# A clustered attention and two MoE layers: a one-hot maximum kept in PSUM, and 1e-9 added by a sum instead of a scalar add

## The chip, the core and the metric

The kernel runs on one core of a Trainium2 chip. The metric is the device time of one execution in microseconds. A core has a matrix engine (TensorE, PE in the rows; its weight loads are listed as PEld), a vector engine (VectorE, DVE), a scalar engine (ScalarE, ACT), a general engine (GpSimd, POOL) and a queue that issues DMAs (SyncE, SP). Each takes its own instructions strictly in order, and they meet at semaphores. SBUF is the large on-chip memory, PSUM the memory that TensorE writes its results into.

## The reference

Three stages follow each other: attention masked by clusters, a dense two-layer MoE expert with a gated unit, and a top-2 MoE over eight experts. The change is in the first alone.

```python
q_assign = np.argmax(np.einsum('bhsd,hcd->bhsc', q_n, c_n), axis=-1)
k_assign = np.argmax(np.einsum('bhsd,hcd->bhsc', k_n, c_n), axis=-1)
mask = q_assign[:, :, :, None] == k_assign[:, :, None, :]
scores = scale * np.matmul(q, k.transpose(0, 1, 3, 2))
scores = np.where(mask, scores, -1000000000.0)
scores = scores - np.max(scores, axis=-1, keepdims=True)
attn = np.exp(scores)
attn = attn / (np.sum(attn, axis=-1, keepdims=True) + 1e-09)
return np.matmul(attn, v).astype(np.float32)
```

There are 2 batches, 8 heads, 768 positions of 64 numbers and 16 clusters.

## The kernel before, in words

**Tiling.** Attention works on eight units, each one batch and one pair of heads. A unit has 12 steps: three groups of query rows (qp), two heads (h), two blocks of 128 rows (i). In a step TensorE makes the scores of 128 queries against 768 keys in two halves (`scores`, L397 and L398), VectorE takes the row maximum (`rowmax`, nm, L403), ScalarE the exponential with its row sum beside it (`expo`, L411), TensorE transposes it (L420), ScalarE and VectorE split it into a high and a low part (PTh, L430; PTl, L435), and TensorE multiplies both with v (`pv`, L455).

**Beside the steps** of one unit the next unit is prepared. Its q and k are transposed and split, their similarity to the clusters is made (simT, then sim in the PSUM tile ps_m, L324), and from that comes a one-hot of the first largest cluster, all on 128 x 384 numbers (24 groups of 16 clusters): the maximum of a group (`c_max`, L330), a compare with it (`c_eq`, L336), a product with falling ranks (`c_rank`, L342, on GpSimd except for the first unit), the maximum of the ranks (`c_first`, m2, L346), and two compares of rank with m2 that write the one-hot oh, one half each (`c_hot`, L353). TensorE transposes oh in six pieces (`h_tr`, L360) into the next user of ps_m, and ScalarE copies it out; four DMAs put it under the q and k operands as the mask.

**The division** runs once per group of query rows, so 24 times: `o_inv` adds 1e-9 to four sums (L480) and takes the reciprocal (L481) into r; GpSimd spreads r over a tile (L485), TensorE transposes that, and GpSimd multiplies it in.

**Order.** A table (TIMES) gives each operation a due time in steps; sorted by it, the operations are written out by hand for all five engines. After attention a scheduler orders what is not written out, the loads of the first dense-layer weights (si, so; L701, L703) and their decoding (L121 to L131) among it. The scores' tile, the transposed tile and the exponential have two buffers each; ps_m has one.

Of the kernel before, what the change touches and what calls it, by code (L numbers as in the profile page):

```python
# [8 lines left out]
F32 = mybir.dt.float32  # L9
# [6 lines left out]
OP = mybir.AluOpType  # L16
AX = mybir.AxisListType
# [3 lines left out]
NCL = 16  # L21
NB = S // 128
# [88 lines left out]
def f(ap):  # L111
    return ap.bitcast(F32)
# [21 lines left out]
class Attention:  # L134
# [52 lines left out]
    def s_set(self):  # L187
        nc = self.nc
        self.ch = self.C([128, H, 2, 2, NCL], F32R, "ch")
        nc.gpsimd.memset(f(self.ch), 0.0)  # L190
        self.zc = self.C([128, 2, 2, 224], F32R, "zc")
        nc.gpsimd.memset(f(self.zc), 0.0)
        self.rev = self.C([128, NCL], F32, "rev")
        nc.gpsimd.iota(self.rev, pattern=[[-1, NCL]], base=NCL, channel_multiplier=0,
                       allow_small_or_imprecise_dtypes=True)
        sb = self.ohsb = self.C([64, 2], F32, "ohsb")
        for p, i, x in ((32, 0, 1.0), (0, 0, PEN), (32, 1, 0.0), (0, 1, -PEN)):
            nc.vector.memset(sb[p:p + 32, i:i + 1], x)
        self.did("set")
# [118 lines left out]
        self.nc.scalar.activation(sT.rearrange("p a n -> p (a n)"), self.t.pop(("simT", u)), AF.Copy)  # L318

    def c_tr(self, u):  # L320
        sim = self.t["sim", u] = self.psm(u, [128, 3, 4, 2, NCL])
        sT = self.t.pop(("sT", u))
        for j in range(3):
            self.nc.tensor.transpose(sim[:, j].rearrange("p g i n -> p (g i n)"), sT[:, j], self.ident)  # L324
# [6 lines left out]

    def c_eq(self, u):
        G = NB * 4
        sv = self.t.pop(("sim", u)).rearrange("p j g i n -> p (j g i) n")
        eq = self.t["eq", u] = self.sm.tile([128, G, NCL], F32, tag="eq", name="eq", bufs=1)
        self.nc.vector.tensor_tensor(eq, sv, self.t.pop(("m1", u)).to_broadcast([128, G, NCL]), op=OP.is_equal)  # L336

# [4 lines left out]
        (self.nc.gpsimd if u else self.nc.vector).tensor_mul(sc, self.t.pop(("eq", u)), self.rev[:, None, :].to_broadcast([128, G, NCL]))  # L342

    def c_first(self, u):
        m2 = self.t["m2", u] = self.sm.tile([128, NB * 4, 1], F32, tag="m2", name="m2", bufs=1)
        self.nc.vector.tensor_reduce(m2, self.g("sc", u), axis=AX.X, op=OP.max)  # L346

    def c_hot(self, u):
        oh = self.t["oh", u] = self.sm.tile([128, 2, 3, 4, NCL], BF16, tag="oh", name="oh", bufs=1)
        scv = self.t.pop(("sc", u)).rearrange("p (j g i) n -> p j g i n", g=4, i=2)  # L350
        m2v = self.t.pop(("m2", u)).rearrange("p (j g i) o -> p j g i o", g=4, i=2)
        for i in range(2):
            self.nc.vector.tensor_tensor(oh[:, i], scv[:, :, :, i], m2v[:, :, :, i].to_broadcast([128, 3, 4, NCL]),  # L353
                                         op=OP.is_equal)
# [50 lines left out]
    def expo(self, j):  # L405
        u, qp, h, i = self.steps[j]
        if (h, i) == (0, 0):
            self.t["sums", u, qp] = self.sm.tile([128, 2, 2], F32, tag="sums", name="sums")
        self.room(2, "P")
        P = self.t["P", j] = self.pp.tile([128, 2, 384], F32, tag="P", name="P")  # L410
        self.nc.scalar.activation(P, self.t.pop(("s", j))[:, :, :384], AF.Exp, bias=self.t.pop(("nm", j)), scale=1.0,  # L411
                                  accum_out=self.g("sums", u, qp)[:, h, i:i + 1])
        self.did("ex", j)

    def trans(self, j, g):
# [61 lines left out]
    def o_inv(self, u, qp):  # L477
        self.need(*(("ex", self.steps.index((u, qp, h, i))) for h in range(2) for i in range(2)))
        r = self.t["r", u, qp] = self.sm.tile([128, 2, 2], F32, tag="r", name="r")
        self.nc.vector.tensor_scalar_add(r, self.t.pop(("sums", u, qp)), 1e-9)  # L480
        self.nc.vector.reciprocal(r, r)  # L481

    def o_rep(self, u, qp):
# [1182 lines left out]
```

## Time and profile before

| | |
|---|---|
| time, median of 3 runs | 912.02 us (911.03 to 912.39) |
| profiled execution | 909.39 us, of which the span from first to last instruction is 907.5 us |
| PE, DVE, ACT, POOL busy over the span | 97%, 63%, 54%, 44% |
| attention with its preparation | about 0 to 290 us of the span |
| mean granted TensorE clock | 0.993 of full speed |

A row of busy time counts an instruction from start to end, so an instruction that waits inside itself for something that the semaphores don't show looks merely long. Matmuls overlap each other and their ends are modelled: two rows of 0.34 us can start 0.18 us apart. The idle time before an instruction is put down to the one whose semaphore came last.

### The profile page before, as it was taken

The page shows a single profiled execution, that of the slowest core. Times are in us where ns is not written, and L with a number is a line of the kernel's source. Part 1 is how long each engine was busy: PE and PEld are TensorE (multiplying, and loading weights), DVE is VectorE, ACT ScalarE, POOL GpSimd, SP SyncE. Part 2 cuts the span into 40 slices and gives each one's busy share as a digit, 9 for nine tenths or more (in the row PEclk, how much of TensorE's full clock was granted, in tenths as well). Part 3 has the DMA queues.
Part 4 walks back from the last instruction along what each step waited for, and adds up shares of the span by engine and source line. Part 5 has one row for each costly group of instructions (what it writes and reads, how often), then busy time and mean ns, then how long its engine had stood idle before and what let it go on. Part 6 is the DMA issues. An engine that isn't in the chain of part 4 may idle for free. (4 is left out here: it accounts for less than half of the span.)

```text
span 907.5 us, 14807 instructions
## 1 busy us (share of the span) xinstructions
PE 878.2 (97%) x5277; PEld 803.3 (89%) x5277; DVE 571.6 (63%) x1133; ACT 487.4 (54%) x1021; POOL 397.2 (44%) x459
## 2 busy tenths in 40 slices
PE   7999999999999999999999999999999999999997
PEld 4898998998888788888999889888889999999996
DVE  3889989999896767667445754582443535445431
ACT  2788888888697566655434544531433334434320
POOL 3134434443654988983000150245424254464632
PEclk9999999999899999999999999999999999999999
DMA  8856766676513343332100160245564456456512
GB/s 218 195 131 179 192 159 173 166 193 187 160 59 111 97 137 116 117 94 70 47 24 24 59 185 35 70 147 171 186 179 141 142 158 187 149 171 196 167 35 69
DMA packets 77531, 120.13 MB, mean 132 GB/s; under 512 B 9858, under 2 KB 55939, under 8 KB 76941
## 3 DMA queue, kind: packets, MB, share of 16 engines
q1 hardware_dynamic: 69997, 100.98, 38.1%
q0 software_dynamic: 7456, 18.16, 6.3%
q8 instruction: 43, 0.70, 0.3%
q14 instruction: 35, 0.29, 0.1%
HBM read 72.85 MB, written 23.76 MB: 106 GB/s over the span
## 5 line engine op out<-in xcount | busy, mean ns | idle before, releaser
L1375 DVE SCALAR_TENSOR_TENSOR hl<-bank,hh 128x240 fp32r<-128x240 f32 (+6 forms) x80 | 40.6, 509 | 131.2 <-ACT hh L1374 131.2
L1374 ACT ACTIVATE hh<-bank 128x240 fp32r<-128x240 f32 (+6 forms) x80 | 35.5, 453 | 162.2 <-PE bank L1366 162.2
L435 DVE TENSOR_TENSOR PTl<-ps_pt,PTh 128x384 fp32r<-128x384 f32 x192 | 98.9, 549 | 12.2 <-ACT PTh L430 11.2
L430 ACT ACTIVATE PTh<-ps_pt 128x384 fp32r<-128x384 f32 x192 | 87.8, 496 | 29.7 <-PE ps_pt L420 28.5
L403 DVE TENSOR_REDUCE nm<-ps_s 128x1 f32<-128x768 f32 x96 | 91.2, 950 | 14.6 <-PE ps_s L398 14.4
L420 PE MATMUL ps_pt<-ident,P 128*128 128x128 f32 x576 | 88.3, 277 | 3.8 <-DVE PTl L435 3.5
L411 ACT ACTIVATE P<-ps_s,nm 128x768 f32<-128x768 f32 x96 | 87.3, 909 | 5.1 <-DVE nm L403 5.1
L1366 PE MATMUL bank<-xT,wB 128*128 128x240 f32 (+3 forms) x480 | 82.1, 318 | 0.0
L420 PEld LDWEIGHTS ps_pt<-ident,P 128*128 128x128 f32 x576 | 68.3, 141 | 14.0 <-DVE PTl L435 11.0
L1366 PEld LDWEIGHTS bank<-xT,wB 128*128 128x128 f32 x480 | 75.9, 188 | 2.2
L823 PE MATMUL bank<-woh,gh 128*128 128x512 f32 x192 | 76.2, 397 | 0.0
L823 PE MATMUL bank<-wol,gh 128*128 128x512 f32 x192 | 75.1, 391 | 0.0
L1136 POOL TENSOR_TENSOR wA<-stg,wA 128x512 fp32r<-128x512 f32 x16 | 20.7, 1296 | 115.9 <-DVE wol L715 54.3
L397 PE MATMUL ps_s<-k,q 128*128 128x384 f32 x192 | 70.6, 368 | 0.4 <-ACT P L411 0.2
L823 PE MATMUL bank<-woh,gl 128*128 128x512 f32 x192 | 70.1, 391 | 0.0
L398 PE MATMUL ps_s<-k,q 80*128 80x384 f32 x192 | 66.3, 345 | 2.6 <-DMA q<-ohT 2.6
L455 PE MATMUL ps_o<-PTh,vs 128*128 128x256 f32 x288 | 53.8, 295 | 0.6 <-ACT PTh L430 0.3
L455 PE MATMUL ps_o<-PTl,vs 128*128 128x256 f32 x288 | 54.0, 296 | 0.0
L1419 PE MATMUL bank<-hh,wA 128*128 128x432 f32 (+2 forms) x192 | 50.4, 354 | 0.2 <-ACT hh L1374 0.2
L1404 POOL DMA_INDIRECT out_dram<-Y,idx x31 | 34.8, 1123 | 35.7 <-DVE Y L1403 27.4
L1048 POOL DMA_INDIRECT xs<-R,rridx x24 | 25.0, 1040 | 52.6 <-DVE rridx L1041 45.9
L778 PE MATMUL bank<-xh,wih 128*128 128x384 f32 x128 | 45.0, 352 | 1.8 <-ACT wih L758 0.9
(324 smaller groups left out, 2326.5 us busy)
## 6 DMA issues: line engine op xcount, KB each, us to landing
stg<-in_moe_w_dram SPq DMA_DIRECT2D x64, 512.0 KB
q<-ABq SPq DMA_DIRECT2D x48, 192.0 KB
k<-ABk SPq DMA_DIRECT2D x48, 192.0 KB
si<-in_moe_w_in_dram SPq DMA_DIRECT2D x14, 512.0 KB
so<-in_moe_w_out_dram SPq DMA_DIRECT2D x14, 512.0 KB
xs<-zrow SPq DMA_DIRECT2D x24, 217.7 KB
ld<-in_k_dram SPq DMA_DIRECT2D x8, 384.0 KB
ld<-in_q_dram SPq DMA_DIRECT2D x8, 384.0 KB
```

Of the source, the lines that this page charges most:

```text
L397: self.nc.tensor.matmul(o, self.g("S1", u, "q")[:, h, qs], self.g("S1", u, "k")[:, h, ks], start=True, stop=False)
L398: self.nc.tensor.matmul(o, self.g("S2", u, "q")[:80, h, qs], self.g("S2", u, "k")[:80, h, ks], start=False, stop=True)
L403: self.nc.vector.tensor_reduce(nm, self.g("s", j)[:, :, :384], axis=AX.XY, op=OP.max, negate=True)
L411: self.nc.scalar.activation(P, self.t.pop(("s", j))[:, :, :384], AF.Exp, bias=self.t.pop(("nm", j)), scale=1.0, accum_out=self.g("sums", u ...
L420: self.nc.tensor.transpose(ps[:, k, :], P[:, k * 128:(k + 1) * 128], self.ident)
L430: self.nc.scalar.activation(self.pt_at(j, g, 0), self.g("pt", j, g), AF.Copy)
L435: self.nc.vector.tensor_sub(self.pt_at(j, g, 1), self.t.pop(("pt", j, g)), f(self.pt_at(j, g, 0)))
L455: self.nc.tensor.matmul(self.g("O", u, qp)[:, h, :], vs[:, h, 2 * i + half].rearrange("p a d -> p (a d)"), PTx[:, kc, :], start=(c == 1 an ...
L778: nc.tensor.matmul(h, w[:, kb, :], x[0][:, kb, sl], start=(n == 0), stop=(n == len(terms) - 1))
L823: nc.tensor.matmul(acc[j], g[:, sl], w, start=(fb == 0 and n == 0), stop=(fb == FB1 - 1 and n == 2))
L1366: self.nc.tensor.matmul(ps, w[:, kb, :], xT[:, kb, x], start=(kb == 0 and i == 0), stop=(kb == KB - 1 and i == 2))
L1419: self.nc.tensor.matmul(ps[d], w[:, sl], a, start=(fb == 0 and n == 0), stop=(fb == FB2 - 1 and n == 2))
```

## The change

m2 no longer has a tile of its own in SBUF. The PSUM tile that holds sim is asked for as a full bank of 512 numbers per partition; sim takes 384, and m2 the 24 behind it. So the tile is held until both compares of `c_hot` have read m2, where before `c_eq` was its last reader.

The row sums no longer lie in a rotating tile. One tile, sums, has for each group of query rows, head and block a pair of numbers: the row sum, which the exponential writes, and a constant 1e-9, written once at the start by GpSimd. A sum over the pairs takes the place of the scalar add.

```diff
+        self.sums = self.C([128, 3, 2, 2, 2], F32, "sums")
+        nc.gpsimd.memset(self.sums, 1e-9)
...
     def c_tr(self, u):
-        sim = self.t["sim", u] = self.psm(u, [128, 3, 4, 2, NCL])
+        ps = self.psm(u, [128, 512])
+        sim = self.t["sim", u] = ps[:, :384].rearrange("p (j g i n) -> p j g i n", j=3, g=4, i=2)
+        self.t["m2", u] = ps[:, 384:384 + NB * 4].rearrange("p (g o) -> p g o", o=1)
...
     def c_first(self, u):
-        m2 = self.t["m2", u] = self.sm.tile([128, NB * 4, 1], F32, tag="m2", name="m2", bufs=1)
-        self.nc.vector.tensor_reduce(m2, self.g("sc", u), axis=AX.X, op=OP.max)
+        self.nc.vector.tensor_reduce(self.g("m2", u), self.g("sc", u), axis=AX.X, op=OP.max)
...
         m2v = self.t.pop(("m2", u)).rearrange("p (j g i) o -> p j g i o", g=4, i=2)
+        self.t.pop(("sim", u))
...
         if (h, i) == (0, 0):
-            self.t["sums", u, qp] = self.sm.tile([128, 2, 2], F32, tag="sums", name="sums")
+            self.t["sums", u, qp] = self.sums[:, qp]
...
-                                  accum_out=self.g("sums", u, qp)[:, h, i:i + 1])
+                                  accum_out=self.g("sums", u, qp)[:, h, i, 0:1])
...
-        self.nc.vector.tensor_scalar_add(r, self.t.pop(("sums", u, qp)), 1e-9)
+        self.nc.vector.tensor_reduce(r.rearrange("p h (i o) -> p h i o", o=1), self.t.pop(("sums", u, qp)), axis=AX.X,
+                                     op=OP.add)
         self.nc.vector.reciprocal(r, r)
```

Two places move. On TensorE, where the one-hot of a unit is transposed, before:

```order
L420 MATMUL ps_pt<-ident,P 128x128 x2
L360 LDWEIGHTS oh [waits DVE_49]
L360 MATMUL ps_m<-identb,oh 64x128
L360 LDWEIGHTS oh
L360 MATMUL ps_m<-identb,oh 64x128
L360 LDWEIGHTS oh
L360 MATMUL ps_m<-identb,oh 64x128
L360 LDWEIGHTS oh [waits DVE_49]
L360 MATMUL ps_m<-identb,oh 64x128
```

And now, at the same place (all lines are four or five further down):

```order
L424 MATMUL ps_pt<-ident,P 128x128 x2
L364 LDWEIGHTS oh [waits DVE_49]
L364 MATMUL ps_m<-identb,oh 64x128 [waits DVE_49]
L364 LDWEIGHTS oh
L364 MATMUL ps_m<-identb,oh 64x128
L364 LDWEIGHTS oh
L364 MATMUL ps_m<-identb,oh 64x128
L364 LDWEIGHTS oh
L364 MATMUL ps_m<-identb,oh 64x128
```

The second wait on VectorE moved from the fourth transpose to the first: ps_m is free only when both compares are done. On SyncE's queue near the end of attention, where Dm and T are the swap of a group's output halves (`o_swap`) and si and so the first weights of the dense layer, before:

```order
L467 DMA Dm<-T 64x256 [waits DMAHW0_49,DMAHW7_49,Activation_49,Pool_49]
L468 DMA Dm<-T 64x256
L701 DMA si_4338<-in_moe_w_in_dram 128x4x128 [waits DVE_49,DMAHW1_49,PE_49,Activation_49]
L703 DMA so_4340<-in_moe_w_out_dram 128x512 [waits DMAHW2_49]
L701 DMA si_4342<-in_moe_w_in_dram 128x4x128 [waits DMAHW3_49]
L703 DMA so_4344<-in_moe_w_out_dram 128x512 [waits DMAHW4_49,PE_49]
L467 DMA Dm<-T 64x256 [waits DMAHW5_49,Activation_49,Pool_49]
L468 DMA Dm<-T 64x256 [waits DMAHW6_49]
```

And now:

```order
L471 DMA Dm<-T 64x256 [waits DMAHW0_49,DMAHW7_49,Activation_49,Pool_49]
L472 DMA Dm<-T 64x256
L471 DMA Dm<-T 64x256 [waits DMAHW3_49,DMAHW1_49,DMAHW4_49,Activation_49,Pool_49]
L472 DMA Dm<-T 64x256 [waits DMAHW2_49]
L706 DMA si_4308<-in_moe_w_in_dram 128x4x128 [waits PE_49]
L708 DMA so_4310<-in_moe_w_out_dram 128x512
L706 DMA si_4312<-in_moe_w_in_dram 128x4x128 [waits DMAHW5_49]
L708 DMA so_4314<-in_moe_w_out_dram 128x512 [waits DMAHW6_49,PE_49]
```

Four weight loads now stand behind the next swap, which waits for ScalarE. On GpSimd the small memset of sums is new, and one decoding operation (L123) moves ahead of two adds of `o_add`. Otherwise every engine keeps its order.

## Rows read from the trace of the kernel before

**Rows 1.** Busy time of each engine by stretch, whole attention and what follows.

```profile
core 0: us, PE busy (x) PEld busy (x) DVE busy (x) ACT busy (x) POOL busy (x), PEclk, DMA share, GB/s
...
140.00:165.00 25.00, 24.18 (x184) 23.19 (x184) 22.51 (x43) 21.11 (x48) 9.21 (x15) 1.00 0.54 142
...
215.00:240.00 25.00, 22.34 (x160) 20.17 (x158) 22.66 (x42) 20.16 (x48) 13.54 (x19) 0.98 0.58 164
...
305.00:420.00 115.00, 114.94 (x562) 99.56 (x561) 83.12 (x109) 68.66 (x133) 101.27 (x79) 1.00 0.34 105
```

**Rows 2.** Groups by line, 24 to 290 us: busy us, mean ns | idle before.

```profile
L353 DVE TENSOR_TENSOR oh<-sc,m 128x192 bf16<-128x192 f32 x14 | 12.0, 899 | 0.0
...
L480 DVE TENSOR_SCALAR r<-sums 128x4 f32<-128x4 f32 x24 | 9.0, 377 | 0.0
```

**Rows 3.** Single lines: shortest, median, longest ns, first and last start.

```profile
L353 DVE TENSOR_TENSOR oh<-sc,m x16: 345/876/1431, 16.6 to 237.9; 128x192 bf16<-128x192 f32 x16
...
L480 DVE TENSOR_SCALAR r<-sums x24: 152/354/728, 35.6 to 287.0; 128x4 f32<-128x4 f32 x24
...
L793 DVE TENSOR_TENSOR gl<-g,gh x32: 546/927/1667, 290.2 to 420.7; 128x384 fp32r<-128x384 f32 x32
...
L435 DVE TENSOR_TENSOR PTl<-ps_pt,PTh x192: 540/549/559, 28.9 to 286.6; 128x384 fp32r<-128x384 f32 x192
...
L346 DVE TENSOR_REDUCE m<-sc x8: 534/544/553, 16.0 to 236.1; 128x24 f32<-128x384 f32 x8
...
L342 DVE TENSOR_TENSOR sc<-eq,rev x1: 557/557/557, 15.4 to 15.4; 128x384 f32<-128x384 f32 x1
```

**Rows 4.** Timeline of the start: start us, us, engine, line, instruction.

```profile
4.46 0.22 DVE L205 TENSOR_REDUCE cenn<-censq 128x1 f32<-128x64 f32 x1
...
16.62 0.63 DVE L353 TENSOR_TENSOR oh<-sc,m 128x192 bf16<-128x192 f32 x2
```

**Rows 5.** Timeline around the one-hot compares of one unit.

```profile
139.17 1.00 POOL L383 TENSOR_TENSOR vs<-ld,vs 128x384 fp32r<-128x384 f32 x1
...
139.38 1.81 DVE L353 TENSOR_TENSOR oh<-sc,m 128x192 bf16<-128x192 f32 x2
...
140.14 0.83 POOL L514 TENSOR_TENSOR xl<-Xn,xh 128x256 fp32r<-128x256 f32 x1
140.44 0.19 PEld L360 LDWEIGHTS <-oh 128*64 128x64 bf16 x3 [0.62 <-DVE oh L353]
...
141.24 0.19 PEld L360 LDWEIGHTS <-oh 128*64 128x64 bf16 x3 [0.61 <-DVE oh L353]
```

**Rows 6.** Waits, 24 to 290 us: total us, times, longest us.

```profile
DVE nm L403 <- PE ps_s L398: 14.4, 23, 1.1
...
DVE PTl L435 <- ACT PTh L430: 11.2, 13, 4.6
...
PE ps_m L360 <- DVE oh L353: 5.8, 13, 1.0
...
ACT P L411 <- DVE nm L403: 5.1, 10, 1.1
```

**Rows 7.** Stretches of 3 us, columns as in Rows 1.

```profile
236.00:239.00 3.00, 1.80 (x12) 1.20 (x12) 3.00 (x6) 2.02 (x5) 1.15 (x1) 1.00 0.41 131
...
242.00:245.00 3.00, 3.00 (x15) 2.90 (x15) 1.90 (x3) 1.40 (x3) 0.87 (x2) 0.50 0.42 77
...
248.00:251.00 3.00, 3.00 (x23) 2.62 (x22) 2.66 (x5) 2.45 (x7) 0.00 (x0) 1.00 0.38 147
...
275.00:278.00 3.00, 3.00 (x24) 2.79 (x24) 2.97 (x6) 2.68 (x8) 2.85 (x5) 1.00 0.99 357
```

**Rows 8.** Timeline of SyncE's queue at the end of attention.

```profile
273.48 0.40 SPq L701 DMA_DIRECT2D si<-in_moe_w_in_dram  x1
...
280.09 0.47 SPq L467 DMA_DIRECT2D Dm<-T  x1
280.61 1.46 SPq L468 DMA_DIRECT2D Dm<-T  x1
```

**Rows 9.** Timeline of ScalarE, first use of a loaded weight.

```profile
291.68 0.66 ACT L121 ACTIVATE dec<-si 128x512 f32<-128x512 f32 x1
```

More of the change, by code (lines that the diff above doesn't have):

```diff
@@ L333, in c_eq @@
         G = NB * 4
-        sv = self.t.pop(("sim", u)).rearrange("p j g i n -> p (j g i) n")
+        sv = self.g("sim", u).rearrange("p j g i n -> p (j g i) n")
         eq = self.t["eq", u] = self.sm.tile([128, G, NCL], F32, tag="eq", name="eq", bufs=1)
```

## The prediction

> **What bounds the kernel now.** I first read the busy time by stretch [rows 1]. In attention three engines are nearly full at once: of 25 us from 140 to 165, PE is busy 24.2, DVE 22.5 and ACT 21.1. None is the bound alone. They pass each step round (scores, maximum, exponential, transpose, split), and with two buffers each, a late instruction on one is soon a hole on the next. After 305 us PE is busy 114.94 of 115 us, so what attention ends earlier is handed on to the end: the kernel ends when PE does.
>
> Then the groups by line and the single lines, to see which instructions are longer than their work. Two stand out, and they are those that the change touches. The compare L353 takes 345 ns at its shortest and 1431 at its longest for one shape; the scalar add L480 takes 152 to 728 ns for four numbers a partition [rows 3]. In 24 to 290 us they sum to 12.0 and 9.0 us [rows 2].
>
> The timeline shows what they wait for [rows 5]. GpSimd starts L383 at 139.17 and ends at 140.17, and starts L514 at 140.14, ending at 140.97. The two compares begin at 139.38 and end together at 141.19; in the first unit, with GpSimd idle, the same pair takes 0.63 us [rows 4]. So the compare stalls under a GpSimd instruction. Which compare stalls is told by its operands: L793, with both inputs in SBUF, ranges from 546 to 1667 ns, while L435, of the same kind and shape but with one input in PSUM, stays within 540 to 559 over 192 executions among the same GpSimd work [rows 3]. L346, a reduce from SBUF, stays within 534 to 553. That is the whole ground for the forecast: the change turns a compare of the L793 kind into one of the L435 kind, and a scalar add into a reduce.
>
> Last the waits [rows 6]: PE idles 5.8 us, in 13 waits, for the compares. Nobody is listed as waiting long for r itself.
>
> **The change part by part.** The profiled execution took 909.4 us, 907.5 of it span; the sum is made against that. The median of the runs is 2.6 us above it, and I add that at the end.
>
> *The compares.* Fourteen of them lie in 24 to 290 us, a pair for each of seven units, 12.0 / 7 = 1.71 us a pair. Without the stall I take the pair of the first unit, 0.63 us, though its m2 was in SBUF; for PSUM in its place the nearest rows are L435 (549, one input in PSUM) and L342 on DVE (557, both in SBUF), which are the same [rows 3]. Saved on DVE: 7 x 1.08 = 7.6 us. Against it stands the moved wait. Before, three of the six transposes ran under the second compare; now all six come after both. Three weight loads of them take 0.19 us [rows 5], so 7 x 0.19 = 1.3 us of TensorE work loses its cover. What is left is 6.3 us at most on the path to the last transpose; PE's own idle time there is 5.8 us, and it can't gain more than that at this place. Queued behind these transposes are the next scores, and on DVE behind the compares the next maximum, so both sides move up together and I count all 5.8 us. From below the term is -1.3 us (the compares stay as they are and the cover is lost), from above 7.6.
>
> [...]
>
> *The maximum m2* is written to PSUM instead of SBUF: 7 reduces of 0.54 us. No row shows a reduce of this kind that writes PSUM. What it reads is the same, so I take nothing; at the 8 ns between L435 and L342 it would be 0.06 us in all, either way.
>
> *The sums.* The reduce of four pairs is not in the trace. L205 reduces 64 numbers to one in 0.22 us, L346 384 to 24 in 0.544; that is 1 ns a number, and 8 numbers come to 0.22 - 0.056 = 0.164 us (an estimate from these two rows). Bounds: 0.152, the shortest scalar add, and 0.22. Saved on DVE: 24 x (0.377 - 0.164) = 5.1 us; by the bounds 3.8 to 5.4. But no one waits for r, only for the maximum queued behind it: ACT waits 5.1 us in all for a maximum, while DVE waits 14.4 us for scores and 11.2 us for the high part [rows 6]. Where DVE then waits anyway, the saving becomes more waiting. I take half, 2.5 us, with ends at 0 and 5.1.
>
> *The clock.* [...] I take half, 1.1 us, with ends at -2.1 (a second fall elsewhere) and 2.1.
>
> *The moved DMAs and GpSimd work.* The loads of si and so were issued at 273.48; behind the swap at 280.09 and 280.61 to 282.07 they start near 282, 8.6 us later [rows 8]. They are 4 x 0.5 MB; at the 357 GB/s of 275 to 278 [rows 7] that is 5.9 us, so they have landed by about 288. The first use is at 291.68 [rows 9]. This end of attention moves as a whole with the swap's source, so the 3.7 us between are the cover, and I take nothing. The new memset of 24 numbers lies at the start, ahead of the first unit; the moved decoding step stands earlier by two adds, which I also cost at nothing.
>
> Sum: 5.8 + 2.5 + 1.1 = 9.4 us. 909.4 - 9.4 = 900.0 profiled, and with 2.6 the median is 902.6 us. By the ends: the largest gain is 7.6 + 5.1 + 2.1 = 14.8 us, 897.2.
>
> **The rivals.**
>
> *The saving is absorbed.* ACT has 21.1 of 25 us of work and stands in every step; PE has 24.2. If they, and not DVE, set the pace, the hole that PE loses at L360 comes back as a wait for ACT or for scores a step later. For it: DVE already waits 25.6 us for the two. Against it: around the compares both PE and DVE stand still at once, and PE's rows overlap (a full 24.2 holds some slack). Half of the first term and nothing else: 2.9 us, 909.1.
>
> *The stall is not the second SBUF input.* If GpSimd holds up any compare that reads SBUF at all, the pair stays at 1.71 us, the wait for both halves now costs its 1.3 us, and the reduce, held up as the add was, takes 0.377 or, as long as L346, 0.544: up to 24 x 0.167 = 4.0 us, half of it on the path. 912.0 + 1.3 + 2.0 = 915.3. It decides from a pair of more than 1.71 - 0.19 = 1.52 us on. Against it stand L435 and L346, neither ever stretched [rows 3]. [...]
>
> *The loads come late.* If they landed more than 3.7 us later than I reckon, the first dense layer would start late by the rest. To lose all of the gain they would have to land 13 us late, at less than a third of the rate seen. With 6 us lost: 908.6.
>
> *The change does not do what it says* in one half: if only the sums come right, 2.5 us less 1.3, 910.8.
>
> **How the numbers follow.** The forecast holds with 0.62, its own range 898 to 906. Absorbed 0.23; the stall elsewhere 0.09; late loads 0.04; one half only 0.02. About 0.2%, 1.8 us, is what a measurement of this kernel can tell from no change. Faster by more: 0.62, 0.21 of the absorbed case, 0.03 of the late loads, sum 0.86. Within it: 0.02 of the absorbed, 0.04 of the stall elsewhere, 0.02 of one half, sum 0.08. Slower: 0.05 of the stall elsewhere, 0.01 of the late loads, 0.06. The range takes in the absorbed case and stops ahead of no change: 898 to 909.8, with one in ten left out above and less below.
>
> **What would show it.** In the profile of the changed kernel L357 (the compare) should lie at 345 to 360 ns throughout, the pair at about 0.63 us; the reduce of the sums at 150 to 220 ns with no spread. PE's wait for oh should fall from 5.8 us to below 1.5, in seven waits and not 13. DVE's idle time before the maximum should grow by the half of the sums' saving that I leave out, some 2.5 us. The clock row near the last unit should stay at 1.00; if it falls again, the time is 1.1 us above the forecast. The loads of si should be issued about 8 us later against the end of attention, with L121 still not waiting. I am wrong if the compares keep their spread, or if they lose it and PE's busy share in 40 to 215 us stays at 24 of 25 with the units no shorter.

## The result, and the profile after

The changed kernel takes 903.26 us (median of four runs, 902.26 to 904.55) against 912.01 us of the kernel before: a ratio of 0.9906, 95% interval 0.9889 to 0.9922, so 8.6 us gained (7.1 to 10.1). The forecast was 902.6. Run again later beside the kernel before, it came to 0.9890 (0.9874 to 0.9906). The kernel before varied from one comparison to the next (medians from 907.4 to 912.0), so below only ratios within one comparison are used.

The two instructions that stood out in [rows 2, 3] have lost their spread. First the groups by line of the changed kernel, 24 to 290 us (busy us, mean ns | idle before):

```profile
L357 DVE TENSOR_TENSOR oh<-sc,ps_m 128x192 bf16<-128x192 f32 x14 | 4.2, 341 | 0.0
L484 DVE TENSOR_REDUCE r<-sums 128x4 f32<-128x8 f32 x24 | 3.6, 149 | 0.0
```

and the single lines (shortest, median, longest ns):

```profile
L357 DVE TENSOR_TENSOR oh<-sc,ps_m x14: 337/342/344, 44.5 to 231.0; 128x192 bf16<-128x192 f32 x14
...
L484 DVE TENSOR_REDUCE r<-sums x24: 143/149/153, 37.0 to 277.4; 128x4 f32<-128x8 f32 x24
```

In the timeline the compares now run straight through the GpSimd work that held them up in [rows 5]:

```profile
136.39 1.00 POOL L387 TENSOR_TENSOR vs<-ld,vs 128x384 fp32r<-128x384 f32 x1
136.59 0.60 DVE L357 TENSOR_TENSOR oh<-sc,ps_m 128x192 bf16<-128x192 f32 x2
...
137.20 0.38 PEld L364 LDWEIGHTS <-oh 128*64 128x64 bf16 x6 [0.17 <-DVE oh L357]
...
137.35 0.73 POOL L519 TENSOR_TENSOR xl<-Xn,xh 128x256 fp32r<-128x256 f32 x1
```

L387 starts first and lasts to 137.39; the pair begins inside it and is done at 137.19, in 0.60 us where it took 1.81. All six weight loads now follow in one piece, after one wait of 0.17 us.

The waits (total us, times, longest; 24 to 284 us), to be held against [rows 6]:

```profile
DVE nm L407 <- PE ps_s L402: 15.6, 24, 1.6
DVE PTl L439 <- ACT PTh L434: 11.6, 15, 4.6
...
PEld L364 <- DVE oh L357: 1.6, 7, 0.6
...
ACT P L415 <- DVE nm L407: 1.1, 2, 1.0
...
PE ps_m L364 <- DVE oh L357: 0.6, 1, 0.6
```

Both windows reach to the end of attention, which comes sooner now. TensorE's wait for the one-hot went from 5.8 us in 13 waits to 0.6 in one, ScalarE's wait for the maximum from 5.1 to 1.1. DVE's own waits grew by only 1.2 and 0.4 us. The weight loads ahead of the transposes waited 1.6 us; in the kernel before it was

```profile
PEld L360 <- DVE oh L353: 8.4, 13, 1.2
```

The stretch from 140 to 165 us, beside [rows 1]:

```profile
140.00:165.00 25.00, 25.00 (x191) 24.35 (x189) 22.14 (x43) 21.35 (x49) 10.32 (x16) 1.00 0.64 157
```

In 25 us TensorE starts 191 matmuls where it started 184, and it is shown busy all the time.

**The length of a unit** is the steadiest measure, because it takes in no start-up, no fall of the clock (it is 1.00 from 44 to 205 us in the first profiles of both kernels) and nothing of the MoE layers. I read it from the row maximum that starts right behind the pair of compares for the second unit, and from the one five units later. The first transposes of the one-hot, which the expectations below go by, are a worse mark for kernels with m2 in SBUF: they start between the two compares, the pair for the second unit is shorter (1.28 us) than the five after it (1.81), and so these kernels are read 0.1 us a unit too short (32.05 before). By the maximum, before:

```profile
44.31 0.94 DVE L403 TENSOR_REDUCE nm<-ps_s 128x1 f32<-128x768 f32 x1
...
205.07 0.94 DVE L403 TENSOR_REDUCE nm<-ps_s 128x1 f32<-128x768 f32 x1
```

After:

```profile
45.01 0.95 DVE L407 TENSOR_REDUCE nm<-ps_s 128x1 f32<-128x768 f32 x1
...
198.48 0.95 DVE L407 TENSOR_REDUCE nm<-ps_s 128x1 f32<-128x768 f32 x1
```

That is (205.07 - 44.31) / 5 = 32.15 us a unit before and 30.69 after: 1.46 us each. All kernels of this study, read in the same way:

| kernel | ratio to before (95%) | a unit, us | against before |
|---|---|---|---|
| before, first and second profile | 1 | 32.15, 32.13 | |
| changed, first and second | 0.9906 (0.9889 to 0.9922), 0.9890 (0.9874 to 0.9906) | 30.69, 30.68 | -1.46 |
| compare only | 0.9911 (0.9890 to 0.9932) | 31.10 | -1.06 |
| sums only | 0.9977 (0.9963 to 0.9991) | 31.77 | -0.38 |
| split of v early, before | 0.9969 (0.9954 to 0.9984) | 31.19 | -0.97 |
| split of v early, changed | 0.9923 (0.9901 to 0.9944) | 30.69 | -1.46 |
| waste ahead of the compares, changed | 0.9961 (0.9940 to 0.9982) | 31.60 | -0.55 |
| waste behind the compares, changed | 0.9923 (0.9904 to 0.9941) | 31.18 | -0.98 |
| decoding late, changed | 0.9859 (0.9841 to 0.9878) | 30.69 | -1.46 |
| decoding late, before | 0.9966 (0.9949 to 0.9984) | 32.14 | -0.01 |
| moved wait alone | 1.0019 (1.0006 to 1.0032) | 32.29 | +0.14 |

Not all that attention gains is seen in the first profile after. Its span is 901.4 us, 6.1 below the 907.5 before, though the first matmul of the dense layer's second product (L823, now L828) comes 9.6 us sooner. Before:

```profile
294.61 0.48 PE L823 MATMUL bank<-woh,gh 128*128 128x512 f32 x1
```

and after:

```profile
284.99 0.48 PE L828 MATMUL bank<-woh,gh 128*128 128x512 f32 x1
```

From 600 to 630 us TensorE stood still more than in the kernel before, as this stretch of the changed kernel shows:

```profile
600.00:630.00 30.00, 27.47 (x180) 23.82 (x179) 9.94 (x52) 4.98 (x15) 13.46 (x24) 1.00 0.55 174
```

The same stretch of the changed kernel's second profile:

```profile
600.00:630.00 30.00, 29.76 (x202) 26.55 (x201) 9.72 (x33) 6.43 (x18) 13.12 (x23) 1.00 0.52 169
```

The loss of 2.3 us did not come again in the second profile, but it is no accident of one execution either. The same stretch of the compare only, described below:

```profile
600.00:630.00 30.00, 27.62 (x171) 23.99 (x170) 10.10 (x53) 4.54 (x13) 15.08 (x26) 0.94 0.56 179
```

In the other profiles TensorE is busy for 27.98 us there (early split, changed) up to 29.77 (before). Whether an attention that ends sooner brings this loss on is open.

### The profile page after: what moved, and what is told of

Same layout as the page of the kernel before. It is cut to its first block, busy times and chain, and to the rows that moved or that the text cites. A ratio compares the mean times of both kernels' runs of the same rounds, so it can differ in the third digit from the quotient of the medians.

```text
span 901.4 us, 14807 instructions
## 1 busy us (share of the span) xinstructions
PE 873.9 (97%) x5277; PEld 801.7 (89%) x5277; DVE 557.6 (62%) x1133; ACT 485.9 (54%) x1021; POOL 395.2 (44%) x460
## 5 line engine op out<-in xcount | busy, mean ns | idle before, releaser
L828 PE MATMUL bank<-woh,gh 128*128 128x512 f32 x192 | 76.1, 396 | 0.0
L828 PE MATMUL bank<-wol,gh 128*128 128x512 f32 x192 | 75.0, 391 | 0.0
L828 PE MATMUL bank<-woh,gl 128*128 128x512 f32 x192 | 70.0, 391 | 0.0
```

Of the source, the lines that this page charges most:

```text
L828: nc.tensor.matmul(acc[j], g[:, sl], w, start=(fb == 0 and n == 0), stop=(fb == FB1 - 1 and n == 2))
```

## The experiments

**Compare only.** The kernel before with m2 in PSUM; the scalar add stays.

```diff
...
+        self.t["m2", u] = ps[:, 384:384 + NB * 4].rearrange("p (g o) -> p g o", o=1)
...
-        m2 = self.t["m2", u] = self.sm.tile([128, NB * 4, 1], F32, tag="m2", name="m2", bufs=1)
...
```

> The kernel before with the compare's edit alone (m2 in PSUM behind sim); the scalar add of 1e-9 stays. Theory (a compare with one input in PSUM is not held up by GpSimd, and DVE's time in attention is worth about 0.85 of itself): the compare falls from a mean of 899 ns to 340 ns, a pair from 1.71 to 0.6 us, 7 x 1.1 x 0.85 = 6.5 us gained, 905.5 us. TensorE's wait for oh falls from 5.8 us to under 1. Rival (absorbed: the gain of the changed kernel is from the sums, or needs both): 909 to 912 us. The scalar add keeps its spread of 152 to 728 ns.

Measured 0.9911 (0.9890 to 0.9932), 8.1 us (6.2 to 10.0) where 6.5 were expected; a unit is 1.06 us shorter. The single lines (shortest, median, longest ns):

```profile
L355 DVE TENSOR_TENSOR oh<-sc,ps_m x14: 341/345/350, 44.6 to 233.6; 128x192 bf16<-128x192 f32 x14
...
L482 DVE TENSOR_SCALAR r<-sums x24: 156/164/745, 37.1 to 279.0; 128x4 f32<-128x4 f32 x24
```

and two of the waits, 24 to 284 us:

```profile
ACT P L413 <- DVE nm L405: 4.9, 9, 1.1
...
PEld L362 <- DVE oh L355: 1.6, 7, 0.6
```

The compare is cured alone, the scalar add still spreads to 745 ns. The gain is the larger part of the change; the rival of 909 to 912 falls. The weight loads' wait for oh went from 8.4 to 1.6 us, ScalarE's wait for the maximum stayed (5.1 and 4.9). In this run's profile the clock stayed at 1.00 near the last unit, so the 8.1 us may hold the clock's part too.

**Sums only.** The kernel before with the pairs and the reduce; m2 stays in SBUF.

```diff
...
-        self.nc.vector.tensor_scalar_add(r, self.t.pop(("sums", u, qp)), 1e-9)
+        self.nc.vector.tensor_reduce(r.rearrange("p h (i o) -> p h i o", o=1), self.t.pop(("sums", u, qp)), axis=AX.X,
+                                     op=OP.add)
...
```

> The kernel before with the sums' edit alone (1e-9 stored beside each sum, a reduce for the scalar add); m2 stays in SBUF. It also has the moved DMA issues and the moved decoding step, which come with this edit. Theory: the reduce takes 149 ns as in the changed kernel, 24 x 0.228 = 5.5 us less on DVE, of which the prediction took half: 2.5 to 2.7 us gained, 909.4; at the share of 0.85 that the changed kernel shows for both edits together, 4.6 us, 907.4. Rival (nobody waits for r, so nothing is gained): 912 us. The compares keep their 345 to 1431 ns.

Measured 0.9977 (0.9963 to 0.9991), 2.1 us (0.8 to 3.4), a unit 0.38 us shorter:

```profile
L482 DVE TENSOR_REDUCE r<-sums x24: 144/150/152, 37.3 to 286.2; 128x4 f32<-128x8 f32 x24
...
ACT P L413 <- DVE nm L405: 1.2, 2, 1.1
```

Of the 3 x 0.228 = 0.68 us of DVE time that three reduces save in a unit, 0.38 come out: 56%. That is the half that the prediction took; the expectation's other share, 0.85, was too high. The two parts add up: 1.06 + 0.38 = 1.44 of the 1.46 us. ScalarE's wait for the maximum, 5.1 us before, fell with this edit.

What held up the scalar add, which the prediction tells by its spread alone, can be read in the kernel before:

```profile
88.41 0.73 POOL L475 TENSOR_TENSOR Xs<-T,Dm 64x256 f32<-64x256 f32 x1
88.54 0.63 DVE L480 TENSOR_SCALAR r<-sums 128x4 f32<-128x4 f32 x1
```

The add ends 0.03 us behind GpSimd's instruction, which began ahead of it. So do all 13 adds of 0.26 us or more; the other eleven take 0.15 to 0.16. Of the 24 reduces of the changed kernel twelve begin and end under a GpSimd instruction, and none is longer than 153 ns.

**The split of v early**, in the kernel before and in the changed one:

```diff
-    "v0": 4.491, "v1": 7.558,
+    "v0": 4.0, "v1": 4.1,
```

> The kernel before, both edits out; only GpSimd's split of v (L382, L383) is written out earlier, so that it no longer runs during the compares of six units. The compare's operands stay in SBUF. Theory (the stall is GpSimd's work beside it, and nothing in the compare itself): L353 falls towards 345 ns where GpSimd is idle; what is left runs beside L514 alone, so a pair takes 0.6 to 1.1 us in six units instead of 1.81; 6 x 0.7 to 1.2 x 0.85 = 3.6 to 6 us gained, 906 to 908.4. Rival (the compare from SBUF is slow of itself in this place, the PSUM operand is what makes it quick): the pair stays at 1.8 us and the time at 912.

> The changed kernel with the same earlier split of v. Theory: the compares already take 340 ns whatever GpSimd does, so nothing is left to gain: 903 us, within 1 us, compares at 340 ns. Rival (the earlier split helps by itself, for instance because GpSimd's rank product or the spread of r comes sooner): as much below the changed kernel as the early split is below the kernel before.

In the kernel before a unit became 0.97 us shorter (0.9969, 0.9954 to 0.9984), with no operand changed. The timeline of a middle unit shows why:

```profile
137.95 0.73 POOL L514 TENSOR_TENSOR xl<-Xn,xh 128x256 fp32r<-128x256 f32 x1 [0.40 <-ACT xh L507]
138.29 0.88 DVE L353 TENSOR_TENSOR oh<-sc,m 128x192 bf16<-128x192 f32 x2
```

Only L514 still runs there. It ends at 138.68; the pair takes 0.88 us, 0.25 above the 0.63 of the first unit [rows 4], instead of 1.81. It became so in five units, not in the six of the expectation: the first and the last of the seven pairs stay at 1.28 and 1.71 us, under other GpSimd work. By the units 5 x 0.97 = 4.8 us are gained; the time shows 2.8 (1.5 to 4.2), less than the 3.6 to 6 expected. In the changed kernel the same move does nothing to a unit (30.69 in both). So the stall of these compares is GpSimd's work beside two SBUF inputs: with one input in PSUM the pair of the middle unit takes 0.60 us, with L383 moved away 0.88. The ratio of the early split in the changed kernel, 0.9923 (0.9901 to 0.9944), overlaps with both of the changed kernel's.

**Waste put back.** In the changed kernel two reduces that nobody reads, on DVE and out of GpSimd's way, once ahead of the compares and once behind them:

```diff
...
+        for k in range(2 if u else 0):
+            junk = self.sm.tile([128, NB * 4, 1], F32, tag="junk", name="junk", bufs=2)
+            self.nc.vector.tensor_reduce(junk, self.rev[:, None, :].to_broadcast([128, NB * 4, NCL]), axis=AX.X, op=OP.max)
...
```

> The changed kernel with two extra reduces on DVE (SBUF, no one reads them, about 0.54 us each, starts 0.46 us apart) just before the compares of seven units: the time that the stall took is put back, without GpSimd. Theory (what counts is DVE's time ahead of the last maximum and of the one-hot): 7 x 0.95 x 0.8 = 5.3 us lost against the changed kernel, 908.5 us, TensorE's wait for oh back at 4 to 6 us. Rival (the PSUM operand or the freed GpSimd brought the gain, not the time on DVE): within 1 us of the changed kernel, 903.

> The same two reduces just behind the compares instead: the one-hot comes as early as in the changed kernel, only the maximum behind it is late. Theory A (TensorE's wait for oh is the price, as the prediction's first term has it): the time stays near the changed kernel, 903 to 904.5, the wait for oh stays under 1 us. Theory B (DVE's time is the price wherever it falls, since the maximum behind the compares is late as well): as the one with the reduces ahead, 908 us, the loss seen as waits for the maximum and the scores.

Ahead of the compares (L363 and L370 are the compare and the transposes there):

```profile
138.91 1.01 DVE L354 TENSOR_REDUCE junk<-rev 128x24 f32<-128x384 f32 x2
...
139.82 0.62 DVE L363 TENSOR_TENSOR oh<-sc,ps_m 128x192 bf16<-128x192 f32 x2
...
140.49 0.49 PE L370 MATMUL ps_m<-identb,oh 128*64 128x128 bf16 x6 [0.89 <-DVE oh L363]
```

The compares start 0.91 us later and a unit is 31.60 - 30.69 = 0.91 us longer: all of it counts, where the expectation took 0.8 of it. TensorE waits for oh again, 6.9 us in the sum of its waits:

```profile
PE ps_m L370 <- DVE oh L363: 6.9, 7, 1.5
```

Behind the compares the same work costs 31.18 - 30.69 = 0.49 us a unit, 54%, and the waits show where:

```profile
PEld ps_pt L430 <- DVE PTl L445: 12.8, 42, 1.2
...
PE ps_m L370 <- DVE oh L362: 0.6, 1, 0.6
```

TensorE no longer waits for oh but, later, for DVE's low parts (7.4 us in the changed kernel, 12.8 here). Neither theory is right whole: DVE time counted in full ahead of an instruction that TensorE waits for, and by about half behind it. In time the two kernels came to 0.9961 and 0.9923, 3.5 us apart; 7 x 0.42 = 2.9 by the units. The loss of the second rests on the unit alone: 0.9923 is also the ratio of the early split in the changed kernel, whose unit is not longer.

**The decoding late.** Four decoding steps of a dense-layer weight are written out later. Two of them run on DVE, one ahead of the last unit's reduce (L125) and one between it and the compares (L127), and now come behind the compares; the GpSimd step that follows them (L131) comes later with them:

```diff
-    "w012": -18.9, "w013": -18.4, "w014": -18.2, "w015": -17.6,
+    "w012": -17.7, "w013": -17.4, "w014": -17.2, "w015": -16.6,
```

> The changed kernel with two decoding steps of a dense-layer weight (L125, L127 on DVE) written out behind the last unit's compares instead of between them; they do the same work. Theory (the clock falls near the last unit because DVE holds TensorE up there, and the changed kernel still has a hole of 0.8 us at L125): the hole goes, the granted clock stays at 1.00 from 216 to 256 us, 1 to 2 us gained, 901.5. Rival (the fall comes whatever DVE does there, or costs nothing): the time at 903 with the clock at 0.50 for 3 us as now.

> The kernel before with the same move of the two decoding steps and nothing else. Theory: the compares' stall of 1.7 us in the last unit remains and holds TensorE up alone; the clock may still fall, and at most 1.5 us is gained: 909.5 to 911. If the clock stays at 1.00 and 2 us or more are gained, the decoding steps and not the compares made the hole, and the prediction's clock term was put at the wrong instruction.

The clock near the last unit, first the changed kernel (columns as in [rows 1]):

```profile
230.00:232.00 2.00, 1.40 (x12) 1.01 (x10) 2.00 (x5) 1.21 (x4) 0.99 (x1) 0.88 0.55 179
232.00:234.00 2.00, 2.00 (x10) 1.88 (x9) 1.43 (x5) 1.77 (x3) 1.92 (x4) 0.50 0.04 8
234.00:236.00 2.00, 2.00 (x14) 1.90 (x14) 0.91 (x2) 0.67 (x4) 1.90 (x3) 0.77 0.37 68
```

then its second profile:

```profile
230.00:232.00 2.00, 1.42 (x12) 1.20 (x13) 2.00 (x5) 1.23 (x3) 1.43 (x2) 1.00 0.52 172
232.00:234.00 2.00, 2.00 (x19) 1.97 (x18) 1.85 (x5) 1.93 (x5) 1.92 (x3) 1.00 0.11 18
```

and the changed kernel with the decoding late:

```profile
230.00:232.00 2.00, 1.90 (x16) 1.64 (x17) 2.00 (x6) 1.86 (x6) 0.00 (x0) 1.00 0.60 193
```

With the decoding late TensorE is busy 1.90 of 2 us where it was 1.40, and the clock stays. L125 itself is shorter there. In the changed kernel it runs beside GpSimd's L346, which lasts from 227.58 to 228.59:

```profile
227.92 0.95 DVE L125 TENSOR_SCALAR dec<-dec 128x512 uint32<-128x512 uint32 x1
```

and with the decoding late beside nothing of GpSimd's:

```profile
231.82 0.42 DVE L125 TENSOR_SCALAR dec<-dec 128x512 uint32<-128x512 uint32 x1
```

So a stall like that of the scalar add was part of the hole that the change left. In the changed kernel itself TensorE does just as little in the stretch (1.40 and 1.42), and the clock fell once and stayed once. With the decoding late the kernel came to 0.9859 (0.9841 to 0.9878) of the kernel before, the quickest of the study, 12.8 us below it; the intervals of this and of the changed kernel's repeat just touch. Against the changed kernel's ratios it is 2.8 to 4.3 us, more than the 1 to 2 expected. From the first maximum to the last it takes 240.0 us, the changed kernel 240.5 with the clock at 1.00 and 242.6 with the fall: in attention 0.5 us is the move's own and 2.1 the fall that stayed away. What the times show beyond that is not explained. In the kernel before, the move left a unit's length alone (32.14) and still gained 0.34% (0.16 to 0.51), 3.1 us, with the clock at 1.00 in its profile: by the expectation's own words the decoding steps, not the compares alone, made that hole. The last unit's compares also ran free of GpSimd there (0.35 us each), so the two are not fully told apart.

Over all thirteen profiles the clock fell near the last unit in seven. With the compares in SBUF and the decoding in place it fell in five of five; with the compares cured, in two of six (the first profile of the changed kernel, and its early split); with the decoding late, in none of two. What decides it is not shown: with the waste ahead of the compares TensorE was busy for only 0.55 of the 2 us from 236 to 238, and the clock stayed at 1.00.

**The moved wait alone.** The kernel before with the two compares in the other order; TensorE's first transpose then waits for both.

```diff
-        for i in range(2):
+        for i in (1, 0):
             self.nc.vector.tensor_tensor(oh[:, i], scv[:, :, :, i], m2v[:, :, :, i].to_broadcast([128, 3, 4, NCL]),
```

> The kernel before with the two compares in the other order, so that TensorE's first transpose of oh waits for both halves, as in the changed kernel, while the compares stay as long as before (m2 in SBUF). Theory (the first term's subtraction): three transposes a unit lose their cover, 0.19 us each unit, a unit of 32.0 us becomes 32.2, 7 x 0.19 = 1.3 us lost. Rival (TensorE catches up before the next scores are wanted): no change in a unit's length, and the 1.3 us should not have been taken off.

A unit is 0.14 us longer, 7 x 0.14 = 1.0 us; the time is 1.0019 (1.0006 to 1.0032), 1.7 us (0.5 to 2.9). The wait is collected in one place:

```profile
PE ps_m L360 <- DVE oh L353: 8.2, 7, 1.7
```

5.8 us in 13 waits became 8.2 in 7. The wait that the change adds has a price, and it agrees with the 1.3 us that were taken off.

**Both kernels again.**

> The changed kernel once more, to see what of its profile comes again: a unit of 30.7 us and a compare of 340 ns should; the fall of the clock near the last unit and the idle time of TensorE at 600 to 620 us need not. Theory: 0.9906 of the kernel before within 0.003. Rival (the first comparison was lucky): above 0.993.

> The kernel before once more, one profile. Theory: the profile read for the prediction was a quick one of its kind, 2.6 us below the median, so that TensorE should now idle some 2 to 3 us more at 530 and between 600 and 630 us, with a unit again at 32.0 us. Rival: the same profile, so that the changed kernel really loses 3.5 us there.

The changed kernel again: 0.9890, within the 0.003 that was expected, a unit of 30.68 us. The kernel before again: 32.13 us a unit, and no extra idle time of TensorE at 600 to 630 us:

```profile
600.00:630.00 30.00, 29.76 (x196) 26.35 (x195) 15.08 (x62) 7.31 (x19) 17.09 (x21) 1.00 0.56 191
```

So the theory of this run fell: the profile read for the prediction was not the odd one there. Its rival, that the changed kernel loses these microseconds each time, doesn't fit the changed kernel's second profile, but with the compare only showing the same loss it is not excluded that the change makes it more frequent.

## Why the prediction was right, point by point

- *The stall is GpSimd's, and the operand decides.* Right, and now shown from both sides: the operand (compare only) and GpSimd's work (split of v early). In the kernel before each of the twelve stretched compares ends 0.21 to 0.22 us behind a GpSimd instruction that began ahead of it. The pair takes 0.60 us against 0.63 reckoned. A single compare is no longer for its input in PSUM: 342 ns with m2 there, 345 ns at the shortest with m2 in SBUF [rows 3].
- *The first term, 5.8 us.* Somewhat too small. In the five middle units the account closes: a pair takes 1.81 - 0.60 = 1.21 us less, the moved wait takes 0.14 of that, and 1.06 came out. With the first pair (1.28 us before) and the last (1.70) reckoned in the same way it is 6.8 us, an estimate from these numbers; the compare alone gained 8.1 us (6.2 to 10.0), with the clock's part in it. The term was capped at TensorE's idle time before the matmuls on oh, 5.8 us; the weight loads ahead of them waited 8.4 us, and 6.8 of that went. That the maximum behind the compares comes sooner, which the prediction counted in, is not seen as a gain of its own: ScalarE waits for it as long as before (4.9 us) until the sums are changed.
- *The moved wait, 1.3 us.* Right: 1.0 us by the units, 1.7 (0.5 to 2.9) by the time.
- *The sums, 2.5 us of 5.1.* Right: 7 x 0.38 = 2.7 us by the units, 2.1 by the time. The path is the one that was named: ScalarE's wait for the maximum went from 5.1 to 1.2 us (sums only). DVE's idle time before the maximum grew by 1.2 us in the changed kernel and 1.6 with the sums only, half to two thirds of the 2.5 that were to show it. The reduce takes 149 ns where I reckoned 164, just under the bound of 152.
- *The clock, 1.1 us of 2.1.* No run shows the term itself, half of a fall; they show a whole one in the first profile of the changed kernel and none in its second. Its size was right. By [rows 7] it is 2 x 3 x (1 - 15 / 23) = 2.1 us, an estimate from 15 matmuls in a stretch of 3 us at 0.50 and 23 in one at 1.00, taken for two stretches. From the first maximum to the last the changed kernel takes 267.5 - 24.9 = 242.6 us with a fall and 265.8 - 25.3 = 240.5 without. The line of its first profile (shortest, median, longest ns, first and last start):

```profile
L407 DVE TENSOR_REDUCE nm<-ps_s x96: 924/947/959, 24.9 to 267.5; 128x1 f32<-128x768 f32 x96
```

  and that of its second:

```profile
L407 DVE TENSOR_REDUCE nm<-ps_s x96: 925/947/959, 25.3 to 265.8; 128x1 f32<-128x768 f32 x96
```

  The term was put in part at the wrong instruction: the compares were only a part of the hole in TensorE's work ahead of the fall; with them cured TensorE still stands (1.40 of 2 us busy), and DVE's decoding step L125 and what follows it are the rest. Nor were both compares of the last unit long, but the second alone, under GpSimd's decoding.

```profile
237.63 0.35 DVE L353 TENSOR_TENSOR oh<-sc,m 128x192 bf16<-128x192 f32 x1
...
237.85 1.26 POOL L131 TENSOR_TENSOR raw<-dec 128x512 f32<-128x512 f32 x1 [1.88 <-DVE dec L127]
...
237.90 1.43 DVE L353 TENSOR_TENSOR oh<-sc,m 128x192 bf16<-128x192 f32 x1
```

  The fall came in two of six profiles with the compares cured and in five of five without; that half of a fall was a fair price is luck.
- *The loads behind the swap, nothing.* Right. The queue and ScalarE in the changed kernel:

```profile
270.48 0.46 SPq L471 DMA_DIRECT2D Dm<-T  x1
270.98 1.07 SPq L472 DMA_DIRECT2D Dm<-T  x1
272.10 0.59 SPq L706 DMA_DIRECT2D si<-in_moe_w_in_dram  x1
```

```profile
282.08 0.66 ACT L121 ACTIVATE dec<-si 128x512 f32<-128x512 f32 x1
```

  The loads leave 1.4 us sooner than in [rows 8], while attention ends 9.6 us sooner: 8.2 us later against it, 8.6 said. L121 has no wait before it.
- *What attention ends earlier is handed on to the end.* Only in part. In the first profiles attention ends 9.6 us sooner and the kernel 6.1, in the second ones (the same matmuls at 293.4 and 283.3, spans of 905.9 and 897.0) 10.1 and 8.9. The forecast for the profiled execution, 900.0 us, was missed by 3.2: it took 903.15. That the median came so close is in part luck, because the 2.6 us between the profile before and its median did not come again after.
- *The absorbed case* did not come, because the saving that TensorE waited for was passed on whole; the half that was lost is that of the sums. The stall elsewhere and the one half only fell too: the compares take 337 to 344 ns, and each edit gains alone.

## What to carry to other kernels

An instruction that is long at one time and short at another, at one shape, may be waiting inside itself: look on the other engine's timeline for one that began ahead of it and ends just before it does. Such a stall was cured here at the operand (one input in PSUM: 0.60 us a pair in place of 1.81; a reduce for a scalar add: at most 153 ns in place of 728) and in the order (the other engine's work moved away: 0.88 us a pair), and the order gave nothing more once the operand was cured (a unit of 30.69 us with it and without). Time taken off VectorE, which is not alone the bound, counted in full (0.91 of 0.91 us a unit) where TensorE, the fullest engine, waits for that instruction, and by about half (54% and 56%) where it doesn't; so price it by who waits.

## What the runs showed of the hardware

- A compare with both inputs in SBUF that began under a GpSimd instruction ended 0.21 to 0.22 us behind it (twelve of the fourteen after 24 us): the pair of [rows 5] took 1.81 us under L383 and L514, 0.88 under the end of L514 alone, 0.60 with one input in PSUM, all of it under L387. The one that began ahead of L131 (237.63) took 0.35 us, the one that began behind it (237.90) 1.43.
- A scalar add on four numbers a partition was held up in the same way and ended 0.03 us behind GpSimd's instruction (13 of 24, up to 728 ns); a reduce in its place took 143 to 153 ns.
- The same hole in TensorE's work, 1.40 and 1.42 us busy of 2, was followed by a granted clock of 0.50 in one execution and by 1.00 in another. One profile does not tell whether a clock fall belongs to a kernel.
- From 232 to 234 us TensorE starts 10 matmuls in the profile with the granted clock at 0.50, 19 in the one at 1.00.
